# Two attention decode blocks, last heads of an output projection: loaded in long rows, laid out, and summed in four column groups

## The chip, the core and the metric

One core of a Trainium2 chip runs the whole kernel. The metric is device time in microseconds (us), the median of several runs; a profile of one execution stands beside it. Engines are named as in the profile: PE (matmul; PEld its weight loads), DVE (vector), ACT (scalar), POOL and SP (it issues most DMAs here).

## What is computed

Two independent blocks, A and B, of single-token attention with caches, of 32 heads, 8192 cached positions and 128 dimensions each; the outputs stand side by side (1 x 1 x 1024):

```python
q = (x @ wq).reshape(1, 1, 32, 128).transpose(0, 2, 1, 3)
scores = jnp.einsum("bhqd,bhkd->bhqk", q, k_cache) * 128 ** -0.5
p = softmax(scores, axis=-1)
o = jnp.einsum("bhqk,bhkd->bhqd", p, v_cache)
y = o.transpose(0, 2, 1, 3).reshape(1, 1, 32 * 128) @ wo        # wo: 4096 x 512
# out = concatenate([y of A, y of B], axis=-1)
```

All inputs are bf16. Each of the four caches has 67 MB, each `wq` and `wo` 4.2 MB.

## The kernel before, in words

The engines' programs are written out by hand, one stream an engine, with semaphores between them. Four heads form a group; 16 groups (8 of A, 8 of B) go through a loop on PE, DVE and ACT each. One group has 8.4 MB of K and 8.4 MB of V. K has two slots in `kn`, V one in `vn`; SP issues the loads in order, each behind the semaphore that frees its slot. In a round DVE multiplies K by q in place (L279), PE adds over the dimensions with matmuls on an identity (L430), DVE reduces to scores (L307) and their maximum, ACT takes the exponential (L379), PE multiplies by V (L483), DVE adds up the four parts of PE's result (L284, L287), PE sums over the partitions (`total_of_group`, L436), and DVE divides (`outs`, L296).

`wo` of A and of B go into the K slot that is free at the end. The loads are issued by SP behind the last V load: A in one piece, B in six, `WOB` (L89). A piece with `rows` true is read as `(p j) n -> p (j n)`: partition p gets `j` whole rows of `wo` in one run, so that with j = 4 it is 4 KB. In this form the rows of one head lie on 128/j partitions, so the heads' outputs have to be laid out accordingly: `spread` (L328, DVE) multiplies them with a mask into `zb`, PE multiplies by a selection `jsel` (L449, `mid`), and `lay` (L336, DVE) copies the result into `o2`. That is done for all heads but the last four, ahead of the last V group. The last four heads of B, 28 to 31, come as three loads in plain rows of 1 KB (2, 1 and 1 heads), and their outputs go straight from the division into `o2` (L347).

Heads of A and heads 0 to 15 of B are multiplied with `wo` by `partial` (L443): 512 columns at a time, head h into column group h mod 4 of `yps[0]` (partitions 0, 32, 64, 96), two rows (A, B) each. ACT copies that to `yc` (L382, semaphore c_ya). Then PE adds the four groups with a selection matrix `sel16`, for A and B at once, into two column groups of `yps[1]` of 256 columns (L496), and adds heads 16 to 31 of B there, two matmuls a head (L505). The last of them raises c_y. DVE copies one half to `out_sb` (L349, c_yd) and ACT the other (L384, c_ya); SP waits for both and stores 2 KB (L232). `turn_over` (L461) are five matmuls without use of their results, between the two parts.

Of the kernel before, what the change touches and what calls it, by code (L numbers as in the profile page):

```python
# [8 lines left out]
BF16 = mybir.dt.bfloat16  # L9
F32 = mybir.dt.float32  # L10

P = 128
# [33 lines left out]
def bass_concat_heads__mha_block_cached__gqa_block_cached__decode_kernel(  # L46
# [41 lines left out]

    WOB = [(0, 16, True), (16, 8, True), (24, 4, True), (28, 2, False), (30, 1, False), (31, 1, False)]  # L89
    RG = [32, 16, 8, 4]  # L90
    NH = NOUT // 2

    with ExitStack() as st:
# [3 lines left out]
        def sb(name, shape, dt):  # L97
            return ec(nc.sbuf_tensor(name, shape, dt))
# [56 lines left out]

        c_pool, c_sel, c_mul, c_sr, c_g, c_gm, c_self, c_st, c_o, c_rl, c_yd = (
            sem(n) for n in ("c_pool", "c_sel", "c_mul", "c_sr", "c_g", "c_gm", "c_self", "c_st", "c_o", "c_rl", "c_yd"))

# [28 lines left out]
        def _(e):  # L187
# [20 lines left out]
            def load_wob(g):  # L208
                h0, n, rows = WOB[g]
                src = wos[1][h0 * Dh:(h0 + n) * Dh, :]  # L210
                dst = kn[:, WO + h0 * NOUT:WO + (h0 + n) * NOUT]
                if rows:
                    src = src.rearrange("(p j) n -> p (j n)", p=P)
                elif n > 1:
                    src = src.rearrange("(j p) n -> p j n", p=P)
                    dst = dst.rearrange("p (j n) -> p j n", j=n)
                e.dma_start(dst, src).then_inc(s_wob[g], 16)

# [13 lines left out]
            e.dma_start(out[0].rearrange("o (a n) -> (o a) n", a=NA), out_sb[:]).then_inc(s_out, 16)  # L232
            e.wait_ge(s_out, 16)
# [9 lines left out]
        def _(e):  # L243
            with once(e):
# [48 lines left out]
                def outs(dst):  # L293
                    w_self()
                    w_ex()
                    e.tensor_tensor(dst, mtp[:, EX:EX + G], rinv[:], ALU.mult).then_inc(c_o, 1)  # L296
# [22 lines left out]

                todo = [(0, 0, H)] + [(1, h0, n) for h0, n, rows in WOB if rows]  # L320
                e.wait_ge(c_o, N)
# [19 lines left out]
                spread(1)  # L341
                for i in range(len(todo)):
                    lay(i)
                    if i + 2 < len(todo):
# [4 lines left out]
                e.tensor_copy(out_sb[:, 0:NH], yps[1][0:NA, 0:NH]).then_inc(c_yd, 1)  # L349


        @block.scalar
        def _(e):
            load_wq(e, 1)
            with once(e):
# [26 lines left out]
                e.copy(yc, yps[0][:]).then_inc(c_ya, 1)  # L382
                e.wait_ge(c_y, 2)
                e.copy(out_sb[:, NH:NOUT], yps[1][HP:HP + NA, 0:NH]).then_inc(c_ya, 1)  # L384


        @block.tensor
        def _(e):
            with once(e):
# [48 lines left out]
                def wo_rows(h):  # L438
                    return kn[:, h * NOUT:(h + 1) * NOUT]

                def partial(h):
                    k = h % G * HP
                    return e.matmul(yps[0][k:k + NA, :], o2[:, h, :], wo_rows(h), start=False, stop=False,  # L443
                                    skip_group_check=True)

                def mid():
                    for i, (a, h0, n) in enumerate([(0, 0, H)] + [(1, h0, n) for h0, n, rows in WOB if rows]):
                        e.wait_ge(c_rl, (1, 2, 4, 6)[i])
                        e.matmul(lay_ps[i][:, 0:n], zb[:, i % 2, :], jsel[n][:], start=True,  # L449
                                 stop=True).then_inc(c_rm, 1)  # L450
# [43 lines left out]
                e.wait_ge(c_ya, 1)  # L494
                for b in range(2):
                    e.matmul(yps[1][b * HP:b * HP + NA, 0:NH], sel16[:, 0, 0:NA],  # L496
                             yc[:, b * NH:(b + 1) * NH], start=True, stop=False, skip_group_check=True)
                for g in range(1, len(WOB)):
                    h0, n, rows = WOB[g]
                    e.wait_ge(s_wob[g], 16)  # L500
                    for h in range(h0, h0 + n):
                        for b in range(2):
                            if h == H - G - 1 and b:
                                e.wait_ge(c_o, N + 1)
                            m = e.matmul(yps[1][b * HP:b * HP + NA, 0:NH], o2[:, H + h, :],  # L505
                                         wo_rows(H + h)[:, b * NH:(b + 1) * NH], start=False,
                                         stop=(h == H - 1), skip_group_check=True)
                m.then_inc(c_y, 1)

# [27 lines left out]
```

## Time and profile before

| | |
|---|---|
| time, median of 3 runs | 665.04 us (664.96 to 666.86) |
| span of the profiled execution, first to last instruction | 663.5 us |
| median over that span | 1.5 us |
| mean granted PE clock in the span | 0.792 |
| DMA read | 285.2 MB, 430 GB/s over the span |
| PE, DVE, ACT busy | 58%, 55%, 12% |

The profiled execution's own time is its span of 663.5 us; what lies around it is not in the profile, and the runs' median is 1.5 us above it. Busy shares are over the whole span. A row of the timeline gives start, length, engine, line, operation, output and input, count, and in brackets the idle time ahead and what ended it; matmul ends are modelled, and consecutive matmuls overlap. Rows of the windows give the stretch, the busy time and count of each engine, the granted PE clock, the DMA engines' share and GB/s. Lines are those of the kernel before.

### The profile page before, as it was taken

Reading aid. Unit: us, or ns where it says so; the run is one execution under the profiler, and the core shown is the slowest. Engines: PE = TensorE matmul, PEld = TensorE weight load, DVE = VectorE, ACT = ScalarE, POOL = GpSimd, SP = SyncE. Lnnn points to the kernel's source line nnn. Section 1 sums busy time; section 2 is a strip of 40 time slices with the busy share of each in tenths; the row PEclk is TensorE's granted clock in tenths of the full one; section 3 lists DMA queues with packets and bytes.
Section 4 is the critical chain, followed back from the end, with each engine's and each line's share of the span. In section 5 each row is a group of like instructions: output and inputs, shape, how many; then the busy total and the mean of one; then the engine's idle time right before and its main releaser. Section 6 shows DMA issues by size and latency. Waiting matters only on the chain.

```text
span 663.5 us, 7942 instructions
## 1 busy us (share of the span) xinstructions
PE 385.8 (58%) x2402; PEld 191.8 (29%) x2402; DVE 362.5 (55%) x249; ACT 76.6 (12%) x212; POOL 2.3 (0%) x12
## 2 busy tenths in 40 slices
PE   0455685854819185481918548191854819185488
PEld 0122232423315042330404233140423314032233
DVE  1009494848292754829274482927548292744821
ACT  0370202020010202001020200102020010202002
POOL 1000000000000000000000000000000000000000
PEclk9995988786959678695967869596786959678697
DMA  9999998999999999999999999999999999999997
GB/s 379 443 442 442 442 442 379 442 442 442 442 442 442 391 431 442 442 442 442 442 399 423 442 442 442 442 442 411 411 442 442 442 442 442 415 407 442 440 444 317
DMA packets 6041, 285.23 MB, mean 430 GB/s; under 512 B 660, under 2 KB 1176, under 8 KB 1304
## 3 DMA queue, kind: packets, MB, share of 16 engines
q1 hardware_dynamic: 5896, 281.03, 98.0%
q10 hardware_dynamic: 144, 4.19, 1.5%
q14 instruction: 1, 0.01, 0.0%
HBM read 285.21 MB, written 0.00 MB: 430 GB/s over the span
## 4 chain that ended last, share of the span: by engine, by line
DMA 72%; PE 22%; DVE 2%; issue 2%; ACT 1%; ACTq 0%; DVEq 0%; SPq 0%
DMA vn<-in_B_v_cache_dram 34%; DMA vn<-in_A_v_cache_dram 34%; PE acc L483 14%; PE rps L430 5%; DMA xrow<-in_B_x_dram 3%; PE yps L413 2%; DVE kn L279 1%; ACT qmem L368 1%; PE yps L443 1%; ACT pt L379 0%; PE yps L505 0%; DVE s_sb L307 0%; PE rps L461 0%; PE misc L478 0%; PE rps L424 0%
## 5 line engine op out<-in xcount | busy, mean ns | idle before, releaser
L279 DVE TENSOR_TENSOR kn<-kn,qmem 128x16384 bf16<-128x16384 bf16 x32 | 276.7, 8688 | 55.2 <-ACT qmem L368 43.0
L430 PE MATMUL rps<-kn,ident 128*128 x1024 | 236.8, 383 | 0.4
L483 PE MATMUL acc<-vn,pt 128*32 128x512 bf16 x1024 | 92.3, 531 | 145.7 <-DMA vn<-in_B_v_cache_dram 75.3
L307 DVE TENSOR_REDUCE s_sb<-rps 128x64 f32<-128x512 f32 x64 | 44.1, 691 | 165.1 <-PE rps L430 165.1
L430 PEld LDWEIGHTS rps<-kn,ident 128*128 128x128 bf16 x1024 | 96.4, 98 | 111.0 <-issue 22.6
L483 PEld LDWEIGHTS acc<-vn,pt 128*32 128x32 bf16 x1024 | 60.3, 127 | 171.1 <-issue 155.9
L374 ACT ACTIVATE negb<-bmp 128x4 f32<-128x4 f32 x16 | 2.8, 173 | 539.7 <-PE bmp L472 539.7
L379 ACT ACTIVATE pt<-s_sb,negb 32x256 bf16<-32x256 f32 x64 | 54.9, 858 | 4.3 <-ACT negb L374 2.9
L478 PE MATMUL misc<-rsum,ones_f 128*128 128x4 f32 x32 | 9.4, 365 | 56.4 <-ACT pt L379 56.4
L284 DVE TENSOR_SCALAR om<-acc,msk 128x128 f32<-128x128 f32 x16 | 5.6, 350 | 42.8 <-PE acc L483 42.8
L478 PEld LDWEIGHTS misc<-rsum,ones_f 128*128 128x128 f32 x32 | 8.0, 312 | 58.6 <-ACT pt L379 57.8
L413 PE MATMUL yps<-vn,xT 128*128 x64 | 17.3, 419 | 6.2 <-ACT qmem L368 4.2
L287 DVE SCALAR_TENSOR_TENSOR om<-acc,msk,om 128x128 f32<-128x128 f32 x48 | 16.8, 351 | 5.9
L470 PE MATMUL mtp<-ident_f,m 128*1 128x128 f32 x32 | 6.1, 270 | 22.6 <-DVE m L312 22.6
L424 PE MATMUL rps<-ones_bf,zrow 1*128 1x1 bf16 x64 | 11.0, 171 | 13.4 <-DVE kn L279 10.8
L424 PEld LDWEIGHTS rps<-ones_bf,zrow 1*128 1x128 bf16 x64 | 5.8, 91 | 40.6 <-issue 40.6
L368 ACT CAST qmem<-yps 32x128 f32 x64 | 16.4, 256 | 7.0 <-PE yps L413 6.3
L379 ACT ACTIVATION_READ_ACCUMULATOR pt<-s_sb,negb 32x1 f32 x64 | 15.9, 249 | 0.0
L399 PE MATMUL misc<-ident,xrow 2*128 2x2 bf16 x4 | 0.3, 166 | 22.8 <-DMA xrow<-in_B_x_dram 22.8
L413 PEld LDWEIGHTS yps<-vn,xT 128*128 x64 | 6.6, 103 | 16.5 <-issue 13.7
L472 PE MATMUL bmp<-gm,ones_f 1*128 1x4 f32 x32 | 6.1, 258 | 7.3 <-DVE gm L314 7.3
L470 PEld LDWEIGHTS mtp<-ident_f,m 128*1 128x1 f32 x32 | 1.4, 80 | 30.5 <-DVE m L312 30.5
(58 smaller groups left out, 57.0 us busy)
## 6 DMA issues: line engine op xcount, KB each, us to landing
vn<-in_B_wq_dram ACTq DMA_DIRECT2D x1, 4096.0 KB, 21.9
vn<-in_A_wq_dram SPq DMA_DIRECT2D x1, 4096.0 KB, 21.7
kn<-in_A_wo_dram SPq DMA_DIRECT2D x1, 4096.0 KB, 27.4
kn<-in_B_wo_dram SPq DMA_DIRECT2D x1, 2048.0 KB, 27.7
kn<-in_B_wo_dram SPq DMA_DIRECT2D x1, 1024.0 KB, 29.7
kn<-in_B_wo_dram SPq DMA_DIRECT2D x1, 512.0 KB, 30.5
kn<-in_B_wo_dram SPq DMA_DIRECT2D x1, 256.0 KB, 30.8
kn<-in_B_wo_dram SPq DMA_DIRECT2D x2, 128.0 KB, 30.6
```

The source lines that it names most:

```text
L279: e.tensor_tensor(k, k, qflat[:, bass.ds(q, Dh)].unsqueeze(1).broadcast_to([P, HM, Dh]), ALU.mult).then_inc(c_mul, 2)
L287: e.scalar_tensor_tensor(om[t % 2][:], acc[:, t * Dh:(t + 1) * Dh], msk[:, t:t + 1], om[(t + 1) % 2][:], ALU.mult, ALU.add).then_inc(*((c_ ...
L307: e.tensor_reduce(s_sb[:, h * HT:(h + 1) * HT], rps[:, h % 2, :].rearrange("p (t d) -> p t d", d=DW), AX.X, ALU.add).then_inc(c_sr, 1)
L368: i = e.copy(qflat[p, bass.ds(r * (2 * Dh) + j * Dh, Dh)], yps[j][p, h * Dh:(h + 1) * Dh])
L379: e.activation(pt[p, 0:T, h], s_sb[p, :], AF.Exp, bias=negb[p, h:h + 1], scale=scale, accum_out=rsum[p, h:h + 1]).then_inc(c_p, 4)
L413: i = e.matmul(yps[j][:], xT[:, bass.ds(x0 + c, 1)].broadcast_to([P, P]), vn[:, bass.ds(w0 + (c * H * Dh + j * G * Dh), G * Dh)], start=(c ...
L424: e.matmul(rps[:, tile, 0:1], zrow[:], ones_bf[0:1, 0:1], start=True, stop=False, skip_group_check=True)
L430: m = e.matmul(ro, ident[:], src, start=False, stop=False, skip_group_check=True)
L443: return e.matmul(yps[0][k:k + NA, :], o2[:, h, :], wo_rows(h), start=False, stop=False, skip_group_check=True)
L470: e.matmul(mtp[0:1, 0:P], m1[:], ident_f[:], start=True, stop=True).then_inc(c_gx, 1)
L478: e.matmul(misc[:, 0:G], ones_f[:], rsum[:], start=True, stop=True)
L483: m = e.matmul(acc[k:k + HP, :], ptf[:, g * W * G:g * W * G + HP], vn[:, g * W * Dh:(g + 1) * W * Dh], start=(g < G), stop=(g >= NG - G))
```

## The change

- The last four heads of `wo` of B are one load of 4 KB rows. Their outputs are laid out like the others: division into `oD`, `spread`, matmul into `bmp`, `lay`.
- Heads 16 to 31 of B are multiplied in four column groups of 128 columns, one row (B) each, in place of two groups of 256 columns with two rows.
- The four column groups of the first part are added for A and B apart (`total`): B into `yps[1]` ahead of heads 16 to 23, A into the second bank of `rps` ahead of the last four heads.
- ACT copies both results, A first, from four partitions (0, 32, 64, 96; the copy covers 97) with 128 columns each; DVE copies none, and c_yd is gone. The store takes four partitions with two runs of 128 each.

```diff
-    WOB = [(0, 16, True), (16, 8, True), (24, 4, True), (28, 2, False), (30, 1, False), (31, 1, False)]
+    WOB = [(0, 16), (16, 8), (24, 4), (28, 4)]
-    NH = NOUT // 2
+    NQ = NOUT // 4
-        out_sb = sb("out_sb", [NA, NOUT], BF16)
+        out_sb = sb("out_sb", [P, NA * NQ], BF16)
-        lay_ps = [misc, yps[1], acc, mtp]
+        lay_ps = [misc, yps[1], acc, mtp, bmp]
# SP
-            e.wait_ge(c_yd, 1)
-            e.wait_ge(c_ya, 2)
-            e.dma_start(out[0].rearrange("o (a n) -> (o a) n", a=NA), out_sb[:]).then_inc(s_out, 16)
+            e.wait_ge(c_ya, 3)
+            e.dma_start(out[0].rearrange("o (a b n) -> b (o a) n", a=NA, b=G),
+                        out_sb[0:P:HP, :].rearrange("b (a n) -> b a n", a=NA)).then_inc(s_out, 16)
# DVE
                 part()
-                outs(o2[:, NA * H - G:NA * H, NA - 1])
-                e.wait_ge(c_y, 2)
-                e.tensor_copy(out_sb[:, 0:NH], yps[1][0:NA, 0:NH]).then_inc(c_yd, 1)
+                outs(oD[:, N * G:N * G + G])
+                e.wait_ge(c_o, N + 1)
+                spread(last)
+                lay(last)
# ACT
-                e.wait_ge(c_y, 2)
-                e.copy(out_sb[:, NH:NOUT], yps[1][HP:HP + NA, 0:NH]).then_inc(c_ya, 1)
+                for a, t in enumerate((rps[:, 1, :], yps[1][:])):
+                    e.wait_ge(c_y, 2 + a)
+                    e.copy(out_sb[0:P - HP + 1, a * NQ:(a + 1) * NQ], t[0:P - HP + 1, 0:NQ]).then_inc(c_ya, 1)
# PE
+                def layout(i):
+                    n = ns[i]
+                    e.wait_ge(c_rl, (1, 2, 4, 6, 9)[i])
+                    e.matmul(lay_ps[i][:, 0:n], zb[:, i % 2, :], jsel[n][:], start=True,
+                             stop=True).then_inc(c_rm, 1)
...
-                for b in range(2):
-                    e.matmul(yps[1][b * HP:b * HP + NA, 0:NH], sel16[:, 0, 0:NA],
-                             yc[:, b * NH:(b + 1) * NH], start=True, stop=False, skip_group_check=True)
+                def total(a, t):
+                    for b in range(G):
+                        m = e.matmul(t[b * HP:b * HP + 1, 0:NQ], sel16[:, 0, a:a + 1],
+                                     yc[:, b * NQ:(b + 1) * NQ], start=True, stop=(a == 0),
+                                     skip_group_check=True)
+                    return m
...
+                def piece(g):
+                    h0, n = WOB[g]
                     e.wait_ge(s_wob[g], 16)
                     for h in range(h0, h0 + n):
-                        for b in range(2):
-                            if h == H - G - 1 and b:
-                                e.wait_ge(c_o, N + 1)
-                            m = e.matmul(yps[1][b * HP:b * HP + NA, 0:NH], o2[:, H + h, :],
-                                         wo_rows(H + h)[:, b * NH:(b + 1) * NH], start=False,
+                        for b in range(G):
+                            m = e.matmul(yps[1][b * HP:b * HP + 1, 0:NQ], o2[:, H + h, 1:2],
+                                         wo_rows(H + h)[:, b * NQ:(b + 1) * NQ], start=False,
                                          stop=(h == H - 1), skip_group_check=True)
-                m.then_inc(c_y, 1)
+                    return m
+
+                total(1, yps[1])
+                piece(1)
+                layout(len(ns) - 1)
+                piece(2)
+                total(0, rps[:, 1, :]).then_inc(c_y, 1)
+                e.wait_ge(c_rl, 10)
+                piece(3).then_inc(c_y, 1)
```

The end of PE's program, from the sum over the column groups on (`sel` is `sel16`, `qmem` holds `yc`, `o` is `o2`; s_wob0 to s_wob5 are the landings of the pieces of `wo` of B; in brackets what an instruction waits for). Before:

```order
L496 MATMUL yps<-qmem,sel 2x256
L505 MATMUL yps<-kn,o 2x256 [waits s_wob1]
L505 MATMUL yps<-kn,o 2x256 x15
L505 MATMUL yps<-kn,o 2x256 [waits s_wob2]
L505 MATMUL yps<-kn,o 2x256 x6
L505 MATMUL yps<-kn,o 2x256 [waits c_o]
L505 MATMUL yps<-kn,o 2x256 [waits s_wob3]
L505 MATMUL yps<-kn,o 2x256 x3
L505 MATMUL yps<-kn,o 2x256 [waits s_wob4]
L505 MATMUL yps<-kn,o 2x256
L505 MATMUL yps<-kn,o 2x256 [waits s_wob5]
L505 MATMUL yps<-kn,o 2x256
```

And now, with lines of the changed kernel:

```order
L502 MATMUL yps<-qmem,sel 1x128 [waits c_ya]
L502 MATMUL yps<-qmem,sel 1x128 x3
L512 MATMUL yps<-kn,o 1x128 [waits s_wob1]
L512 MATMUL yps<-kn,o 1x128 x31
L449 MATMUL bmp<-jsel,zb 128x4 [waits c_rl]
L512 MATMUL yps<-kn,o 1x128 [waits s_wob2]
L512 MATMUL yps<-kn,o 1x128 x15
L502 MATMUL rps<-qmem,sel 1x128 x4
L512 MATMUL yps<-kn,o 1x128 [waits s_wob3,c_rl]
L512 MATMUL yps<-kn,o 1x128 x15
```

Heads 16 to 31 take 64 matmuls where they took 32, a layout stands ahead of heads 24 to 27, the sum for A stands ahead of the last four heads, and one landing (s_wob3) stands where there were three.

The end of DVE's program, from the reciprocal of the last group on (`oD` holds the divided outputs, `zb` the spread ones, c_y is PE's last result). Before:

```order
L287 SCALAR_TENSOR_TENSOR om<-acc,msk,om 128x128
L291 RECIPROCAL rinv<-misc 128x4 [waits c_o]
L296 TENSOR_TENSOR o<-mtp,rinv 128x4 [waits c_ex,c_self]
L349 CAST out_sb<-yps 2x256 [waits c_y]
L244 REGISTER_ALU
```

And now:

```order
L286 RECIPROCAL rinv<-misc 128x4 [waits c_o]
L291 TENSOR_TENSOR oD<-mtp,rinv 128x4 [waits c_ex,c_self]
L324 TENSOR_TENSOR zb<-oD,mask 128x128 [waits c_rm,c_o]
L332 CAST o<-bmp 128x4 [waits c_rm]
L239 REGISTER_ALU
```

The copy of the result is gone from DVE's end, and a multiply and a small copy for the last four heads stand there.

More of the change, by code (lines that the diff above doesn't have):

```diff
@@ L154, in bass_concat_heads__mha_block_cached__gqa_block_cached__decode_kernel @@
         s_k = [sem("s_k%d" % i) for i in range(2)]
-        c_pool, c_sel, c_mul, c_sr, c_g, c_gm, c_self, c_st, c_o, c_rl, c_yd = (
-            sem(n) for n in ("c_pool", "c_sel", "c_mul", "c_sr", "c_g", "c_gm", "c_self", "c_st", "c_o", "c_rl", "c_yd"))
+        c_pool, c_sel, c_mul, c_sr, c_g, c_gm, c_self, c_st, c_o, c_rl = (
+            sem(n) for n in ("c_pool", "c_sel", "c_mul", "c_sr", "c_g", "c_gm", "c_self", "c_st", "c_o", "c_rl"))
         c_qa, c_nb, c_p, c_ya = (sem(n) for n in ("c_qa", "c_nb", "c_p", "c_ya"))
@@ L208, in load_wob @@
             def load_wob(g):
[L209 to L217, printed above, removed]
+                h0, n = WOB[g]
+                e.dma_start(kn[:, WO + h0 * NOUT:WO + (h0 + n) * NOUT],
+                            wos[1][h0 * Dh:(h0 + n) * Dh, :].rearrange("(p j) n -> p (j n)", p=P)
+                            ).then_inc(s_wob[g], 16)
             load_k(0)
@@ L317, in _ @@
                         outs(oD[:, bass.ds(r * G, G)])
-                todo = [(0, 0, H)] + [(1, h0, n) for h0, n, rows in WOB if rows]
+                todo = [(0, 0, H)] + [(1, h0, n) for h0, n in WOB]
+                last = len(todo) - 1
                 e.wait_ge(c_o, N)
@@ L341, in _ @@
                 spread(1)
-                for i in range(len(todo)):
+                for i in range(last):
                     lay(i)
-                    if i + 2 < len(todo):
+                    if i + 2 < last:
                         spread(i + 2)
                 part()
-                outs(o2[:, NA * H - G:NA * H, NA - 1])
-                e.wait_ge(c_y, 2)
-                e.tensor_copy(out_sb[:, 0:NH], yps[1][0:NA, 0:NH]).then_inc(c_yd, 1)
+                outs(oD[:, N * G:N * G + G])
+                e.wait_ge(c_o, N + 1)
+                spread(last)
+                lay(last)
         @block.scalar
@@ L444, in partial @@
                                     skip_group_check=True)
+                ns = [H] + [n for h0, n in WOB]
+                def layout(i):
[3 more added lines that the diff above has]
+                             stop=True).then_inc(c_rm, 1)
                 def mid():
[L447 to L450, printed above, removed]
+                    for i in range(len(ns) - 1):
+                        layout(i)
                     e.matmul(yps[0][:], zrow[:], ones_bf[0:1, 0:1].broadcast_to([1, 512]), start=True,
```

3 lines of the change are left out of this document (1 added, 2 removed).

## The prediction

> **What bounds the kernel now.** I read the page's first parts, then the chain of work that ended last, then the timeline of the last microseconds.
>
> ```profile
> span 663.5 us, 7942 instructions
> PE 385.8 (58%) x2402; PEld 191.8 (29%) x2402; DVE 362.5 (55%) x249; ACT 76.6 (12%) x212; POOL 2.3 (0%) x12
> DMA  9999998999999999999999999999999999999997
> DMA 72%; PE 22%; DVE 2%; issue 2%; ACT 1%; ACTq 0%; DVEq 0%; SPq 0%
> q14 instruction: 1, 0.01, 0.0%
> ```
>
> The DMA engines are full in every slice but the last, and 72% of the chain is DMA: the caches stream in at the pace of the memory, and nothing that the change touches lies in that stream. All of it lies behind the last cache block. So I price only the tail, from the chain in order of time and the timeline (start, length, engine, line; in brackets the idle time before and who ended it).
>
> ```profile
> 652.58 4.28 PE acc L483 x46
> 656.87 0.86 PE yps L443 x11
> 657.73 1.19 PE rps L461 x5
> ```
> ```profile
> 656.70 1.03 PE L443 MATMUL yps<-kn,o 128*2 128x512 bf16 x16
> ...
> 658.76 0.38 PE L436 MATMUL mtp<-selh,om 128*128 128x4 f32 x2
> ...
> 659.08 0.60 PE L496 MATMUL yps<-qmem,sel 128*2 128x256 f32 x4
> 659.25 0.16 DVE L296 TENSOR_TENSOR o<-mtp,rinv 128x4 bf16<-128x4 f32 x1 [0.46 <-PE mtp L436]
> 659.29 1.40 PEld L505 LDWEIGHTS yps<-kn,o 128*2 128x2 bf16 x24
> 659.51 2.37 PE L505 MATMUL yps<-kn,o 128*2 128x256 bf16 x32
> 660.94 0.09 PEld L505 LDWEIGHTS yps<-kn,o 128*2 128x2 bf16 x4 [0.25 <-DMA kn<-in_B_wo_dram]
> 661.31 0.08 PEld L505 LDWEIGHTS yps<-kn,o 128*2 128x2 bf16 x2 [0.28 <-DMA kn<-in_B_wo_dram]
> 661.60 0.08 PEld L505 LDWEIGHTS yps<-kn,o 128*2 128x2 bf16 x2 [0.21 <-DMA kn<-in_B_wo_dram]
> 661.92 0.36 ACT L384 CAST out_sb<-yps 2x256 bf16<-2x256 f32 x1 [3.55 <-PE yps L505]
> 661.92 0.41 DVE L349 CAST out_sb<-yps 2x256 bf16<-2x256 f32 x1 [2.50 <-PE yps L505]
> 662.37 0.27 SPq L232 DMA_DIRECT2D out_dram<-out_sb  x1
> ```
>
> The chain calls the end PE work without a gap from 652.58 on. The timeline tells more: the reader is to see three short waits for `wo` of B, before heads 28 and 29, before 30 and before 31 (660.94, 661.31, 661.60), 0.7 us together. The last one decides: 0.32 us later (661.92) the copies begin, the longer ends at 662.33, the store is issued at 662.37 and the span ends at 663.5. The whole stretch that can change is 659.1 to 663.5, 4.4 us. The sum is made against this execution: span 663.5; the runs' median, 665.04, lies 1.5 us above it, and I carry differences of the span over to it.
>
> **Part 1, the last four heads in one load of 4 KB rows.** Three loads in 1 KB rows become one. The rate in stretches of 8 KB rows, 4 KB rows and 1 KB rows, in that order (the last number is GB/s):
>
> ```profile
> 655.90:658.00 2.10, 2.10 (x38) 0.81 (x31) 0.82 (x3) 0.21 (x1) 0.00 (x0) 1.00 1.01 421
> 658.40:659.30 0.90, 0.90 (x9) 0.42 (x8) 0.44 (x3) 0.00 (x0) 0.00 (x0) 1.00 1.02 411
> 659.65:660.65 1.00, 1.00 (x24) 0.84 (x20) 0.00 (x0) 0.00 (x0) 0.00 (x0) 1.00 1.11 363
> ```
>
> The last 524 KB take 524/363 = 1.44 us as 1 KB rows and 524/411 = 1.28 us as 4 KB rows: the last byte is 0.16 us earlier, so PE is released at 661.45 in place of 661.60. Bounds: no gain if the end is set by a fixed completion time, 0.2 us at most. I take -0.15. SP issues two loads fewer; it had issued all of them 30 us before they were needed, so that counts nothing.
>
> What is lost is that work could begin on parts. Before, 2 matmuls stood behind the last landing; now 16 do (4 heads by 4 column groups). For their pace I have two rows. In L443, also four column groups, the last of 16 matmuls ends 0.38 us after its start, so three steps of four matmuls with 512 columns take 1.03 - 0.38 = 0.65 us, 0.217 a step; at 128 columns that is 0.054 a head. From above, the shortest matmuls of the trace:
>
> ```profile
> 22.76 0.21 PEld L399 LDWEIGHTS misc<-ident,xrow 2*128 2x128 bf16 x4 [22.76 <-issue]
> 22.79 0.26 PE L399 MATMUL misc<-ident,xrow 2*128 2x2 bf16 x4 [22.79 <-DMA xrow<-in_B_x_dram]
> L399 PE MATMUL misc<-ident,xrow 2*128 2x2 bf16 x4 | 0.3, 166 | 22.8 <-DMA xrow<-in_B_x_dram 22.8
> ```
>
> Four of 2 columns take 0.26 us, the last 0.17 of it: 0.03 a matmul with its weights, 0.12 to 0.13 a head of four. Before, 24 weight loads, 12 heads, take 1.40 us, 0.12 a head. I take 0.06, near L443, which has the same column groups. Three heads then stand between release and the last one: +0.18 (0.16 to 0.39). The last matmul itself is shorter: 512 columns are recorded at 379 ns and 256 at 272, so 128 are about 218, -0.05.
>
> ```profile
> L443 PE MATMUL yps<-kn,o x48: 379/631/634, 648.5 to 657.4; 128*2 128x512 bf16 x48
> L505 PE MATMUL yps<-kn,o x32: 270/272/273, 659.5 to 661.6; 128*2 128x256 bf16 x32
> ```
>
> **Part 2, laying these heads out.** DVE now runs one more multiply and one more copy and PE a matmul between them. The same steps of the earlier groups:
>
> ```profile
> 646.28 0.16 DVE L296 TENSOR_TENSOR oD<-mtp,rinv 128x4 f32 x1 [0.91 <-PE mtp L436]
> 646.52 0.49 DVE L328 TENSOR_TENSOR zb<-oD,mask 128x128 bf16<-128x128 bf16 x2
> 646.88 0.19 PE L449 MATMUL misc<-jsel,zb 128*128 128x32 bf16 x1 [0.75 <-DVE zb L328]
> 647.10 0.20 DVE L336 CAST o<-misc 128x32 bf16<-128x32 f32 x1
> ```
>
> From the head division to the spread heads is 646.28 to 647.30, 1.02 us. From 659.25 this ends at 660.27 if PE is free at once. On PE it stands behind the total for B and heads 16 to 23. The total: L496's four passes hold PE from 659.08 to 659.51; half the columns in four groups take about half, to 659.30. Eight heads at 0.06 end at 659.78, at 0.13 at 660.34. The new wait of PE (for DVE's multiply, ready at 659.25 + 0.60 = 659.85) holds up heads 24 to 27 and the total for A behind it, by 0.1 us; the layout matmul costs 0.2. Heads 24 to 27 then run from about 660.2, when their 4 KB rows have come, to 660.5 (slow pace 661.2), the total for A to 660.7 (661.5). All that has the wait for the last rows, 661.45, as its cover: 0.7 us to spare at the pace I take, none at the slow one. Where the cover is gone (slow pace, and 0.2 us at each of three changes between kinds of matmul, most of the 0.32 from L436's start to L496's, in which L436 has two passes of 4 columns), the last piece starts near 661.9, ends at 662.6, and the span is 0.5 longer. I count 0 and keep 0.5.
>
> **Part 3, one copy and the store.** DVE's copy of 0.41 us and ACT's of 0.36 become two of ACT, of which one runs while PE waits. The other has 128 columns:
>
> ```profile
> L368 ACT CAST qmem<-yps x64: 254/256/258, 27.0 to 47.7; 32x128 f32 x64
> ```
>
> 0.25 for 0.41: -0.16. ACT's first copy (0.25) ends by 661.0; at the slow pace by 661.8, still before 661.9. The store moves 2 KB as eight rows of 256 B from four partitions in place of two of 1 KB. No row shows a store like it. What is there is 0.27 us of issue and a final wait:
>
> ```profile
> SPq L233 <- DMA out_dram<-out_sb: 0.9, 1, 0.9
> ```
>
> Bounds: -0.05 (shorter rows over more engines) to one issue more, +0.27; I take +0.05, near the row, as the bytes are the same. [...]
>
> **Sum.** -0.15 + 0.18 - 0.05 + 0 - 0.16 + 0.05 = -0.13 us: span 663.4, time 664.9. The bounds of these terms, with the PE case, are -0.3 to +0.8: 664.7 to 665.8. The runs of before themselves reach from 664.96 to 666.86; with that I set the lower end at 664.4.
>
> **Rivals.**
> *Slower: PE's program outgrows what it keeps at hand.* Counted over the order (loops once, a matmul with its weight load as two, an fp32 one as four) PE has 443 instructions before and 534 after; the 91 are all at the end: 8 fp32 and 64 bf16 matmuls, a layout and a wait for 2 and 32 of before (32 + 128 + 2 + 1 - 8 - 64). The row of q14 speaks against: one instruction packet in the whole span, while PE's loop ran 16 times; all 443 stayed at hand. It says nothing of 534. It decides if the room lies between 443 and 534: then the last piece waits for a fetch. Its price from rows: 1.2 us (662.37 to 663.5, the round trip of a small transfer) to 2.7 (that, behind the 1.5 us of `wo` that are still under way). 666.1 to 667.6; more if it also empties the loop's own start, for which no row has a price. [...]
> [...]
> *The change doesn't do what it says:* the last rows land no earlier, since a completion time and not the rows sets 661.60. Then the term of -0.15 goes: 665.05. Against it: the waits of 660.94, 661.31 and 661.60 come 0.3 to 0.4 apart, and 131 KB at 363 GB/s take 0.36, so the rate sets them.
> Faster by 2 us would need the chain from 661.45 to 663.5 to vanish; no term reaches it.
>
> **How the numbers follow.** Forecast, 664.9 within its bounds: 0.58. Landing no earlier: 0.07. The store's second trip: 0.07. Room for the program: 0.26, of which 0.14 for one fetch (666.1 to 667.6) and 0.12 for more. Faster by chance of the 660 us ahead of the tail: 0.02. The range 664.3 to 667.4 leaves out the 0.12, the 0.02 and some 0.05 at its two ends; the forecast alone would have 664.4 to 665.8. A difference within 0.3%, 2.0 us, is about what a measurement of this kernel can tell from no change. Over 667.04 lie the 0.12 and about 0.05 of the single fetch: slower 0.17. Faster 0.02, same 0.81.
>
> **What would show it.** Right: one wait for `wo` of B before the last 16 matmuls, ending near 661.4; those 16 within 0.25 us; a last ACT copy of 0.25; the store issued near 662.2; q14 still at one packet. Wrong: 16 matmuls over 0.4 us apart (pace); PE busy without a wait for DMA before the last piece (cover gone); a final wait on the store over 1.5 us (second trip); instruction packets inside the span with PE idle behind no semaphore (room).

## The result: 2.5 us slower, by a late DMA engine and a store that took twice as long

The changed kernel takes 667.50 us (median of 5 runs, 667.19 to 669.55), the kernel before in the same session 665.04 us (5 runs, 664.96 to 666.86): a ratio of 1.0039, 95% interval 1.0028 to 1.0049. That is outside the forecast range of 664.3 to 667.4 by 0.1 us, and on the side (slower) to which the prediction gave 0.17. The profiled execution of the changed kernel took 667.38 us, with a span of 666.1 against 663.5.

The page of the changed kernel: the span, the DMA engines in 40 slices, the rows of the instruction queues (packets, MB, share) and the chain.

```profile
span 666.1 us, 8028 instructions
...
DMA  9999998999999999999999999999999999999996
...
q8 instruction: 1, 0.02, 0.0%
q14 instruction: 1, 0.01, 0.0%
...
DMA 77%; PE 16%; issue 3%; ACT 1%; DVE 1%; SPq 0%; ACTq 0%; DVEq 0%
```

The DMA engines are still full up to the last slice. One row is new: an instruction packet of queue q8. Where it is, and what follows the next load, is in the trace's DMA view for 86 to 89 us and for 99.9 to 101.0 us:

```profile
q1 hardware_dynamic: 16, 1.05, 81.8%
q8 instruction: 1, 0.02, 2.0%
```
```profile
DMA packets 2, 0.07 MB, mean 60 GB/s; under 512 B 1, under 2 KB 1, under 8 KB 1
```

The packet of q8 has 16,384 B, starts at 87.39 us and lasts 0.95 us. Of the 16 data packets of 65,536 B that end at 87.29 to 87.59 us, 15 are followed by the next one by 87.58; one has no successor before 88.32, when the instruction packet is nearly over (88.34). The traces do not name the 16 DMA engines; I read this as one of them being held. In the next load, 15 landing marks come by 99.82 us; one data packet and its mark are still to come, at 100.90. From there on one landing in 16 comes 0.95 to 1.08 us behind the other 15 in every cache load up to 632 us; one of the last big loads ends at 623.33 us (15 of its marks by 622.28). Before, all 16 came within 0.5 us, and that load ended at 621.93: 1.40 earlier. At the end of the program the windows show it plainly; the last two numbers are the DMA engines' share and GB/s. The changed kernel first, then the kernel before:

```profile
661.40:662.30 0.90, 0.61 (x24) 0.32 (x24) 0.00 (x0) 0.00 (x0) 0.00 (x0) 1.00 0.07 27
```
```profile
661.40:662.30 0.90, 0.46 (x4) 0.08 (x2) 0.38 (x1) 0.36 (x1) 0.00 (x0) 1.00 0.00 0
```

A share of 0.07 is one engine of 16: it alone is still loading, while before there was nothing left to load. The timeline of the changed kernel's end:

```profile
657.89 0.53 PEld L441 LDWEIGHTS yps<-kn,o 128*2 128x2 bf16 x16 [0.36 <-DMA kn<-in_B_wo_dram]
...
660.24 0.40 PE L502 MATMUL yps<-qmem,sel 128*1 128x128 f32 x8
...
660.41 0.16 DVE L291 TENSOR_TENSOR oD<-mtp,rinv 128x4 bf16<-128x4 f32 x1 [0.46 <-PE mtp L434]
660.45 0.63 PE L512 MATMUL yps<-kn,o 128*1 128x128 bf16 x32
660.61 0.29 DVE L324 TENSOR_TENSOR zb<-oD,mask 128x128 bf16<-128x128 bf16 x1
661.01 0.10 PEld L449 LDWEIGHTS bmp<-jsel,zb 128*128 128x128 bf16 x1
661.01 0.18 PE L449 MATMUL bmp<-jsel,zb 128*128 128x4 bf16 x1
661.23 0.17 DVE L332 CAST o<-bmp 128x4 bf16<-128x4 f32 x1 [0.33 <-PE bmp L449]
...
661.66 0.40 PE L512 MATMUL yps<-kn,o 128*1 128x128 bf16 x16 [0.47 <-DMA kn<-in_B_wo_dram]
...
662.95 0.39 PE L512 MATMUL yps<-kn,o 128*1 128x128 bf16 x16 [0.67 <-DMA kn<-in_B_wo_dram]
663.39 0.27 ACT L382 CAST out_sb<-yps 97x128 bf16<-97x128 f32 x1 [0.78 <-PE yps L512]
663.68 0.65 SPq L226 DMA_DIRECT2D out_dram<-out_sb  x1
```

The reader is to see two things. PE now waits for `wo` of B before heads 0 to 15 already (657.89), and again before heads 24 to 27 and 28 to 31: nothing of PE's own is in the way, only the late engine. And the store's issue takes 0.65 us, not 0.27. SP's final wait on the store, from the view of waits, is 1.7 us where it was 0.9:

```profile
SPq L228 <- DMA out_dram<-out_sb: 1.7, 1, 1.7
```

The two profiled executions against each other, in us (the landing is the last 4-byte mark of the last load, the first matmul counts from its weight load, the copy's start is that of the last ACT copy, and the end is the start of SP's last wait instruction, 0.02 us before the span ends):

| | before | after | difference |
|---|---|---|---|
| last landing | 661.09 | 662.31 | +1.22 |
| to the first matmul behind it | 0.51 | 0.61 | +0.10 |
| to the last copy's start | 0.32 | 0.47 | +0.15 |
| to the store's issue (the copy) | 0.45 | 0.29 | -0.16 |
| from the issue to the end | 1.16 | 2.41 | +1.25 |
| span | 663.55 | 666.11 | +2.56 |

So two numbers are to be explained: 1.2 us at the landing (the 1.40 of the stream, less 0.18 for the faster last rows) and 1.25 us at the store. The rest, on which most of the prediction's working went, comes to +0.09. Single traces of one kernel differ in the last landing, but the two kinds do not overlap: in the eight traces of this document with a q8 packet near 87 us it comes at 662.31 to 663.32, in the nine without one at 661.04 to 661.88.

### The profile page after: what moved, and what is told of

Same layout as the page of the kernel before. It is cut to its first block, busy times and chain, and to the rows that moved or that the text cites. A ratio compares the mean times of both kernels' runs of the same rounds, so it can differ in the third digit from the quotient of the medians.

```text
span 666.1 us, 8028 instructions
## 1 busy us (share of the span) xinstructions
PE 380.8 (57%) x2442; PEld 190.9 (29%) x2447; DVE 362.6 (54%) x250; ACT 76.8 (12%) x213; POOL 2.3 (0%) x12
## 4 chain that ended last, share of the span: by engine, by line
DMA 77%; PE 16%; issue 3%; ACT 1%; DVE 1%; SPq 0%; ACTq 0%; DVEq 0%
DMA vn<-in_A_v_cache_dram 35%; DMA vn<-in_B_v_cache_dram 35%; PE acc L487 13%; DMA kn<-in_B_wo_dram 5%; DMA xrow<-in_B_x_dram 3%; PE yps L411 2%; PE rps L428 1%; ACT qmem L365 1%; DVE kn L274 1%; ACT pt L376 0%; DVE s_sb L302 0%; SPq L210 0%; ACTq L365 0%; ACTq L43 0%; PE misc L482 0%
## 5 line engine op out<-in xcount | busy, mean ns | idle before, releaser
L487 PE MATMUL acc<-vn,pt 128*32 128x512 bf16 x1024 | 88.4, 514 | 148.8 <-DMA vn<-in_B_v_cache_dram 76.8
L291 DVE TENSOR_TENSOR oD<-mtp,rinv 128x4 f32 (+1 forms) x16 | 2.6, 162 | 14.1 <-PE mtp L434 14.1
```

The source lines that it names most:

```text
L487: m = e.matmul(acc[k:k + HP, :], ptf[:, g * W * G:g * W * G + HP], vn[:, g * W * Dh:(g + 1) * W * Dh], start=(g < G), stop=(g >= NG - G))
```

## The experiments on the late DMA engine

My theory: PE's longer program is fetched in part, and the fetch costs no stall of PE but the place of one DMA engine in the stream. The rival: the changed loads or the new matmuls at the end make the lag. Instructions are counted as in the prediction, 443 before and 534 after; times are medians, with the difference to the kernel before in the same session.

**Code that never runs, at the end of PE's program before.**

```diff
                 m.then_inc(c_y, 1)
+                with e.If(e.snap(by_round) == 1):
+                    for i in range(46):
+                        e.matmul(rps[:, 0, 0:1], ident[:], kn[:, 0:1], start=True, stop=True)
```

With 46 such matmuls (538 instructions):

> The kernel before, with 46 matmuls at the end of PE's program in a branch that is never taken: PE's program grows by 95 instructions to 538 and does nothing more. Theory (the program's length costs a fetch inside the span, whose 16 KB packet sets one of the 16 DMA engines back for good): one instruction packet of 16 KB in the span, one landing of each load about 1.3 us after the other 15, time 666.3 us (+1.3). Rival (the lag of the changed kernel comes from its loads or its timing): no such packet, 665.0.

Measured: 666.21 us (665.98 to 667.65), +1.03, ratio 1.0017 (1.0008 to 1.0026); the packet is there, at 87.17 us, and one landing in 16 is late as in the changed kernel:

```profile
q8 instruction: 1, 0.02, 0.0%
```

So length alone does it, without one instruction more being executed but the branch. With 20 matmuls (486 instructions):

> The same branch with 20 matmuls: 486 instructions, between before (443) and the change (534). [...] If any code added at the end costs a fetch, or the branch itself costs time: 666.3.

Measured: 666.18 us (665.96 to 666.91), +1.00, ratio 1.0017 (1.0008 to 1.0026), with the same packet at 87.26 us. So the limit, if the length sets it, lies below 486.

**The changed kernel without heads 16 to 23 of B** (470 instructions):

```diff
                 total(1, yps[1])
-                piece(1)
                 layout(len(ns) - 1)
```

> The changed kernel without the products of heads 16 to 23 of B (they are left out of the sum): 470 instructions on PE. These matmuls stand in the cover of a landing, so that leaving them out saves nothing by itself. Theory: no packet in the span, the last landing 1.3 us earlier, 666.2 us (667.5 before this edit). Rival (lag from the one long load or from chance): 667.5.

Measured: 667.52 us (667.29 to 668.24), +2.34; the packet is at 87.22. That is the time which the rival foretold. It does not bring the rival back, since the padded kernels have the lag without any change of loads; with the length as the cause, the limit lies below 470. With 4 matmuls of padding, 454:

> The kernel before with 4 matmuls behind a condition that is never true at the end of PE's program: 454 instructions by my count. The packet comes between 443 (none) and 470 (there). If the limit lies near 448: a 16 KB instruction packet near 87 us and one landing of 16 about 1.3 us behind, time about 666.2. If it lies at 460 or more: none, 665.2.

Measured, in one execution: no packet near 87 us and all 16 landings together, span 664.2. But the time was 668.8, 4.6 us more than the span, and a 16 KB packet of q8 stands at 666.17, 2.0 us behind the span's end. So, if the count alone decides, the limit for the fetch inside the stream lies between 454 and 470. The packet behind the end is taken up below.

**The changed kernel without heads 16 to 27 of B** (438 instructions, fewer than before):

```diff
                 total(1, yps[1])
-                piece(1)
                 layout(len(ns) - 1)
-                piece(2)
                 total(0, rps[:, 1, :]).then_inc(c_y, 1)
```

> The changed kernel without the products of heads 16 to 27 of B (left out of the sum): 438 instructions on PE, five fewer than before. All loads, the layout, the last four heads, the copies and the store stay. Theory (the fetch comes with any program longer than that of before): no packet of 16 KB in the span, no landing behind the others, 667.5 - 1.2 = 666.3 us; the store still takes 2.4 us. Rival (the fetch belongs to the changed program's form): packet and 667.5.

Measured: 666.93 us (666.31 to 667.78), +1.86, ratio 1.0027 (1.0017 to 1.0037). In the profiled execution the packet of q8 is gone from the stream, all 16 landings come together again (the last at 661.09 us, as in the kernel before), and the span is 665.1, 1.0 less than after. The median is 0.6 above the expected 666.3, which only the four shortest runs show (666.31 to 666.44): in the others up to 2.35 us lie around the span, where the runs of the kernel before in that session had 1.2 to 1.5. In the trace a q8 packet stands at 666.48, behind the span.

Such a packet behind PE's last branch stands in five traces: with 4 matmuls of padding, without heads 16 to 27 (here, and in the run below with the store of zeros), and in two forms of the changed kernel below, the one that stores zeros and the one in which DVE makes the last copy. Where it lies behind the span (the first, this one and the changed kernel that stores zeros), 4.6, 2.0 and 2.0 us lie around the span; in the other 13 profiled executions whose time is known beside their span, 1.2 to 1.4. That the late packet lengthens the end fits these, but no run tests it; and what makes it come is open: of the kernels with 534 instructions two have it and two do not.

**The loop's hint left out** (the kernel before, 442 instructions; each engine's whole program stands in a loop of one round that was marked as jumping back):

```diff
-            return nc.Fori(0, e.snap(one), engines=[e.engine], hint_back_edge=True)
+            return nc.Fori(0, e.snap(one), engines=[e.engine])
```

> The kernel before with its loop's hint on the back edge left out on all engines (442 instructions on PE by my count). Theory A, the fetch is a matter of the program's length alone: no packet near 87 us, 665.1 +- 0.4. Theory B, the hint is what keeps the loop's code at hand at 443 instructions: packets of instructions inside the span, 666 or more.

Measured: 666.16 us (665.98 to 667.47), +1.00, ratio 1.0015 (1.0006 to 1.0025). Both queues now fetch inside the stream, q14 at 82.53 and q8 at 87.25 us, two of the 16 landings are late (by 0.8 and 1.3 us), and no packet follows at the end. So length is not all: at nearly the same length the hint decides too.

## The experiments on the store

**The changed kernel with a store of two runs of 1 KB,** from a tile of zeros, the result's copies unchanged:

```diff
+            e.memset(out_2k[:], 0.0).then_inc(c_pool, 1)
...
-            e.dma_start(out[0].rearrange("o (a b n) -> b (o a) n", a=NA, b=G),
-                        out_sb[0:P:HP, :].rearrange("b (a n) -> b a n", a=NA)).then_inc(s_out, 16)
+            e.dma_start(out[0].rearrange("o (a n) -> (o a) n", a=NA), out_2k[:]).then_inc(s_out, 16)
```

> The changed kernel with the store of before: two rows of 1 KB, from a tile of zeros, so that the result itself is not stored. All waits stay. Theory (short rows and their number make the store 1.25 us longer, 2.41 from issue to the end for 1.16): 667.5 - 1.25 = 666.25 us. Rival (the store was late for SP's own instruction packet, which stood ahead of it): 667.4.

Measured: 666.13 us (665.93 to 667.64), +0.95, ratio 1.0017 (1.0008 to 1.0026); the store takes 1.17 us again, and the late engine remains (last landing at 663.04). With the store alone changed, 1.4 to 1.5 us are gone.

**Both costs taken away** (without heads 16 to 27, and the store of zeros):

> The same, with the store of before (two rows of 1 KB from a tile of zeros; the result itself is not stored). Theory: both costs gone, and what is left is the change as forecast: 665.0 us within 0.3, last landing 0.15 earlier than before. Rival (a third cost, in the tail's work): 665.8 or more.

Measured: 665.45 us (664.84 to 665.89), +0.38, ratio 1.0004 (0.9995 to 1.0013). Within what a measurement can tell, that is the kernel before: the two costs are nearly the whole loss. In its trace the last landing is not 0.15 earlier, as I had expected, but 0.79 later than in the kernel before (661.88); all 16 came together, and the load that ended at 621.93 there ends at 622.43 here, so most of this lag was there before the tail began.

**What in the store?** First I held the short runs responsible. In the kernel before, with `out_sb` padded so that the two partitions give eight runs of 256 B:

```diff
-            e.dma_start(out[0].rearrange("o (a n) -> (o a) n", a=NA), out_sb[:]).then_inc(s_out, 16)
+            e.dma_start(out[0].rearrange("o (a b n) -> (o a) b n", a=NA, b=G), out_sb[:, :, 0:P]).then_inc(s_out, 16)
```

> The kernel before, with its two result rows padded in the on-chip tile, so that the same two partitions are stored as eight runs of 256 B. [...] Rival (four partitions, not short rows, cost it): 665.2.

Measured: 666.45 us (666.02 to 667.98), +1.38; store 2.30 us. And with four runs of 512 B (`b=2`, halves of 256 columns):

> The same with a pad after 256 columns: four runs of 512 B. [...] Rival (each run costs, whatever its length): about a third of the way, 665.6.

Measured: 666.35 us (666.11 to 667.29), +1.28; store 2.41 us. Runs of 512 B cost as much as runs of 256 B, so I took the length not to be it. What the length alone costs these two stores do not tell, since both met the fetch that is found further down; a store of 256 B runs that did not meet it is shown there (1.73 us, 0.02 us a run). Then the form, three dimensions in place of two? The changed kernel with one run of 512 B from each of the four partitions (in two dimensions, the columns landing in another order):

```diff
-            e.dma_start(out[0].rearrange("o (a b n) -> b (o a) n", a=NA, b=G),
-                        out_sb[0:P:HP, :].rearrange("b (a n) -> b a n", a=NA)).then_inc(s_out, 16)
+            e.dma_start(out[0].rearrange("o (b n) -> (o b) n", b=G), out_sb[0:P:HP, :]).then_inc(s_out, 16)
```

> The changed kernel, but its 2 KB leave as four runs of 512 B, one from each of the four partitions (a plain form of two dimensions), in place of eight runs of 256 B in three dimensions; they land in another order. The instruction packet at 87 us remains. Theory 1, the form of the transfer costs the 1.2 us (its issue, 0.65 to 0.78 us): issue 0.27, store 1.2 us, time 666.2 +- 0.3 (as with two runs of 1 KB, 666.13). Theory 2, the number of runs or partitions costs it: store 2.3 to 2.5 us, time 667.4 +- 0.3.

Measured: 667.90 us (667.50 to 668.25), +2.74; issue 0.60, store 2.49 us. Not the dimensions either.

**The variant that should have had no loss** kept the last four heads in 4 KB rows and in four column groups, but with two result rows a group, heads 16 to 27 multiplied like heads 0 to 15 (512 columns at a time), without the five matmuls of `turn_over`, with four copies (two of DVE, two of ACT) and the old store of two runs of 1 KB. Of its edit:

```diff
-            e.wait_ge(c_ya, 3)
-            e.dma_start(out[0].rearrange("o (a b n) -> b (o a) n", a=NA, b=G),
-                        out_sb[0:P:HP, :].rearrange("b (a n) -> b a n", a=NA)).then_inc(s_out, 16)
+            e.wait_ge(c_yd, 1)
+            e.wait_ge(c_ya, 2)
+            e.dma_start(out[0].rearrange("o (a n) -> (o a) n", a=NA), out_sb[:]).then_inc(s_out, 16)
...
-                        for b in range(G):
-                            m = e.matmul(yps[1][b * HP:b * HP + 1, 0:NQ], o2[:, H + h, 1:2],
...
+                    for b in range(G):
+                        m = e.matmul(yps[1][b * HP:b * HP + NA, 0:NQ], o2[:, H + h, :],
...
```

> What the change brought, without its two costs: the last four heads of wo of B in one load of 4 KB rows, laid out, in four column groups of 128, but with two rows a group; heads 16 to 27 as the first 16 (512 columns); four copies into two partitions, store of two runs of 1 KB. PE has 440 instructions by my count (before 443). Theory (fetch and store are the whole loss): no instruction packet near 87 us, all 16 landings of a load together, store 1.2 us, 665.0 +- 0.4: no gain over before beyond what a measurement tells. Rival (the tail itself is slower): 665.8 or more.

Measured: 666.80 us (666.12 to 667.20), +1.64, ratio 1.0023 (1.0014 to 1.0032). No fetch of PE, all landings together, and yet the loss remains. Two rows of its timeline and one of its waits tell why:

```profile
661.38 0.60 PE L511 MATMUL yps<-qmem,sel 128*2 128x128 f32 x8 [0.69 <-ACT qmem L383]
...
663.07 0.27 SPq L227 DMA_DIRECT2D out_dram<-out_sb  x1
```
```profile
SPq L228 <- DMA out_dram<-out_sb: 2.0, 1, 2.0
```

PE waits for ACT's copy of the column sums, which now comes behind heads 24 to 27 (the store is issued 0.7 us later than before). But above all, the very store that took 1.16 us before, with its issue of 0.27, takes 2.31 us here. With this the theory of the store's form falls as the whole cause.

**A new theory.** I laid the packets of these stores beside each other, in us from the store's issue (data: start of the first and the last data packet; zeros: the changed kernel that stores zeros; four copies: the variant just shown):

```
                     issue  q14's packet     first data  last data  end
before               0.27   +1.16 to +1.66   +0.74       +0.77      +1.16
zeros, 2 x 1 KB      0.27   +1.19 to +1.64   +0.74       +0.78      +1.17
after, 8 x 256 B     0.65   +1.25 to +1.60   +1.28       +1.61      +2.41
without heads 16-27  0.65   +1.54 to +1.85   +1.28       +1.86      +2.70
before, 8 x 256 B    0.78   +1.14 to +1.62   +1.42       +1.66      +2.30
before, 4 x 512 B    0.78   +1.15 to +1.63   +1.41       +1.65      +2.41
after, 4 x 512 B     0.60   +1.26 to +1.77   +1.23       +1.77      +2.49
four copies          0.27   +0.94 to +1.49   +0.74       +1.49      +2.31
```

In each store of over 2 us the last data goes out within 0.04 us of the end of q14's packet of 8 KB, as if it had waited for it. In the two stores of 1.2 us the data is through before. And q14's packet comes 1.41 to 1.48 us after the end of ACT's branch out of its loop (1.70 in one case), whatever PE, DVE and SP do. So my theory: q14 is ACT's instruction queue, its packet is a fetch of ACT once out of its loop, and the store loses a place to that fetch. ACT leaves when its last copy has started (in the changed kernel the copy starts at 663.39 us and the branch ends at 663.53), so the fetch, at 664.94, falls where the store goes out (first data at 664.96). Three runs test it against the form of the store.

**The changed kernel with DVE making the last copy,** store unchanged:

```diff
+                e.wait_ge(c_y, 3)
+                e.tensor_copy(out_sb[0:P - HP + 1, NQ:2 * NQ], yps[1][0:P - HP + 1, 0:NQ]).then_inc(c_yd, 1)
...
-                for a, t in enumerate((rps[:, 1, :], yps[1][:])):
-                    e.wait_ge(c_y, 2 + a)
-                    e.copy(out_sb[0:P - HP + 1, a * NQ:(a + 1) * NQ], t[0:P - HP + 1, 0:NQ]).then_inc(c_ya, 1)
+                e.wait_ge(c_y, 2)
+                e.copy(out_sb[0:P - HP + 1, 0:NQ], rps[0:P - HP + 1, 1, 0:NQ]).then_inc(c_ya, 1)
```

> The changed kernel, its store of eight runs of 256 B and PE's fetch at 87 us as they are; only the last copy (128 columns) is DVE's in place of ACT's, so that ACT leaves its loop about 1.0 us earlier. Theory 1, ACT's fetch at its loop's end stands in the store's way: the packet of q14 comes near 663.9, a microsecond before the store's packets; store 1.7 us from issue to end (first packet 1.28, the rest 0.1, then 0.34 to SP) in place of 2.41; time 666.8 +- 0.3. Theory 2, the form of the store alone: store 2.4 us, time 667.5 +- 0.3.

Measured: 666.93 us (666.57 to 669.48), +1.68, ratio 1.0036 (1.0021 to 1.0050); span 665.7. q14 starts at 664.11 us, 1.45 after the end of ACT's branch, and is over at 664.52; the data goes out from 665.23 to 665.32, and the store takes 1.73 us, as the new theory has it.

```profile
663.57 0.29 DVE L349 CAST out_sb<-yps 97x128 bf16<-97x128 f32 x1 [1.93 <-PE yps L514]
663.95 0.65 SPq L227 DMA_DIRECT2D out_dram<-out_sb  x1
```
```profile
SPq L229 <- DMA out_dram<-out_sb: 1.1, 1, 1.1
```

The issue is still 0.65, the wait behind it 1.1 in place of 1.7. That splits the 1.25 us: 0.57 (1.73 against 1.16) belong to the store's own form, with a first packet at +1.28 in place of +0.74; 0.68 (2.41 against 1.73) to meeting the fetch. The split rests on one trace of each. Each of the eight runs of 256 B takes 0.02 us here, and SP's wait ends 0.36 us after the last mark, 0.34 in the kernel before: of the second trip to which the prediction gave 0.07 there is no sign.

The DMA view of this kernel from 662 to 667 us also has a packet of PE's queue:

```profile
q8 instruction: 1, 0.02, 1.3%
```

It lasts from 664.69 to 665.76 us, over the whole time of the store's data, and holds none of it (nor does one at 663.64 to 664.57 us in the kernel with both costs taken away). So a fetch at the same moment is not enough. That both must fall on the same DMA engine is my guess; the traces do not name the engines.

**The variant with four copies, all of them on DVE:**

> The variant with four copies and a store of two runs of 1 KB (666.8, store 2.31), with all four copies on DVE: 0.57 us more of copying on the path, and ACT leaves its loop after the copy of the column sums, near 660.8. Theory 1 (ACT's fetch): q14 near 662.2, the store takes 1.16 us again, time 666.8 + 0.57 - 1.15 = 666.2 +- 0.3. Theory 2 (something else in this variant's store): 2.3 us, 667.4 +- 0.3.

Measured: 666.73 us (665.83 to 668.22), +1.48, ratio 1.0023 (1.0014 to 1.0031). q14 goes to 662.54 us and the store takes 1.17 us.

```profile
662.64 1.18 DVE L348 CAST out_sb<-yps 2x128 bf16<-2x128 f32 x4 [2.67 <-PE yps L512]
663.85 0.27 SPq L226 DMA_DIRECT2D out_dram<-out_sb  x1
```
```profile
SPq L227 <- DMA out_dram<-out_sb: 0.9, 1, 0.9
```

The store is as foretold, the time is not: 0.2 above the expected range. The copies ended 0.8 us later (0.6 for the copies, 0.2 for PE's result) and the store 1.1 shorter; the span's median over the runs fell only from 665.4 to 665.0, and the median time hardly.

**The kernel before, its store a little later:** DVE's copy of 256 columns in four of 64.

```diff
-                e.tensor_copy(out_sb[:, 0:NH], yps[1][0:NA, 0:NH]).then_inc(c_yd, 1)
+                for b in range(4):
+                    i = e.tensor_copy(out_sb[:, b * NH // 4:(b + 1) * NH // 4],
+                                      yps[1][0:NA, b * NH // 4:(b + 1) * NH // 4])
+                i.then_inc(c_yd, 1)
```

> The kernel before with DVE's last copy of 256 columns cut into four of 64, so that the same store of two runs of 1 KB is issued 0.4 to 0.5 us later and ACT's fetch stays where it is (about 1.45 us after ACT's branch). Theory 1 (ACT's fetch): the store's packets meet the fetch, the store takes 2.2 to 2.4 us in place of 1.16, time 665.1 + 0.45 + 1.1 = 666.7 +- 0.4. Theory 2 (the form of the store alone): 1.16 us, time 665.6 +- 0.3.

Measured: 666.36 us (665.14 to 667.63), +1.11, ratio 1.0017 (1.0008 to 1.0026).

```profile
662.03 0.60 DVE L350 CAST out_sb<-yps 2x64 bf16<-2x64 f32 x4 [2.52 <-PE yps L508]
662.67 0.27 SPq L232 DMA_DIRECT2D out_dram<-out_sb  x1
```
```profile
SPq L233 <- DMA out_dram<-out_sb: 2.1, 1, 2.1
```

The copies take 0.2 us longer, less than I had put in, and the same store of two runs of 1 KB takes 2.36 us: first data at +0.75, q14's packet from +1.20 to +1.51 (this time 1.70 us after ACT's branch), last data at +1.51. Nothing about the store has changed but its moment. The meeting alone costs 1.2 us here, more than the delay that brings it about.

One thing does not fit a plain queue behind the packet. The second data packet was due at +0.77, as before, and q14's packet begins 0.43 us later: the data is held ahead of the packet's own record. Counted from the end of ACT's branch, second packets of such a store that went out up to 1.10 us behind it were free (six traces), and those due at 1.26 and 1.27 us (the variant with four copies, and this kernel) were held. The kernel before, at 1.09, escapes by less than 0.2 us. What holds the engine in that time is not in the trace.

## Why the prediction was wrong, point by point

- **Landing of the last rows, -0.15.** The rate was right: the marks of one engine for the last 524 KB lie 1.25 to 1.27 us apart, about 1.45 before, -0.18. The step that failed is the premise under this term, that nothing the change touches lies in the stream of the caches. The change made PE's program longer, and an instruction packet came into that stream at 87.39 us: from there on one landing of 16 was 0.95 to 1.08 us behind, and the last landing came 1.22 later. In the padded kernels that packet is worth about 1.0 us of time. (The row of slices that I read as full up to the last also has one 8; nothing hangs on that.)
- **The rival on PE's program.** It had the right condition, a limit between 443 and 534 (454 to 470, if the count alone decides), and 0.26. Its price was wrong: a stall of PE before the last piece, 1.2 to 2.7 us. The runs show no such stall, but the lag of one engine. That its span of times, 666.1 to 667.6, takes in the measured 667.50 is luck: half of the loss came from the store.
- **The row of q14.** I read it as PE's own record, which showed that all 443 instructions stayed at hand. It was ACT's: it moves with ACT's branch (the copies on DVE) and not with PE's, and it stands at 663.54, in the last 0.02 us of the span. PE's queue is q8: code on PE alone, never run, made it appear. The row spoke neither for nor against.
- **The size of that room.** That PE keeps a certain number of instructions at hand was my own picture; the runs show only when a packet comes, not what PE holds. The packet has 16,384 B, and the limit for it in the stream lies between 454 and 470 by my count, if the count alone decides. The changed kernel has one packet in 16 rounds, at 87.39 us, and none when PE leaves its loop for the code behind it. Whether that packet brings code for the first time or again is not in the traces, so that they give no size of a room.
- **Pace, +0.18 and -0.05.** 16 matmuls take 0.39 us, one 0.22: 0.17 for the steps, 0.13 for three heads (forecast 0.18). Right, a little generous.
- **Layout, 0.** From the division at 660.41 to the laid-out heads at 661.40 is 0.99 us (forecast 1.02), and behind it PE waited 0.47 and 0.67 us for DMA. The cover held. The late engine does not explain that: it held up PE's start into this stretch (657.89, before 656.70) by as much as the last landing. The whole kernel without the lag was not tried.
- **Copy, -0.16.** 0.265 us in place of 0.41. Right.
- **Store, +0.05.** This term failed as well. "The bytes are the same" was the reason, and the bounds ended at one issue more, +0.27. It was +1.25: 0.57 for a longer issue and a later first packet, 0.68 for meeting ACT's fetch. A second trip, which has 0.07 among the chances, is shown by no run: without the fetch each run of 256 B took 0.02 us, and SP's wait ended 0.36 us after the last mark (0.34 in the kernel before). Its sign, a final wait on the store over 1.5 us, came (1.7) and meant something else. Nor does any run show shorter rows going over more engines, the reason given for the lower bound of -0.05.
- **The range.** It reached to 667.4 by way of a single fetch, so that it missed by only 0.1 us is no merit of the sum. That lag and a slow store would both come was not among the cases; each was priced as if the other did not exist.

## What to carry to other kernels

In a kernel whose DMA engines are full, ask of every longer program whether it brings an instruction packet into the stream: here it came with 534 instructions on PE by my count (not with 443), stalled no engine (PE's next matmuls ran from 87.53 us, while the packet lasted to 88.34), but left one landing of 16 behind by 0.95 to 1.08 us in every cache load up to 632 us, and the last landing came 1.22 us later than before. At the end of a program look at what else is on the DMA engines just then: here the instruction packet of q14 came 1.41 to 1.48 us (1.70 in two cases) behind ACT's branch out of its loop (with the loop's hint), and a store that met it paid 0.7 to 1.2 us, so let that engine be done early, or the store be out first. The small transfer of this kernel was priced by its moment and its issue, not by its bytes.

No version here beats the kernel before in time. What the change wins in the tail itself, 0.18 for the rows and 0.16 for the copy, less 0.25 between landing and copy, is about 0.1 us, which no measurement of this kernel would show.

## What the runs showed of the hardware

- Fetches of PE are one packet of 16 KB (0.93 to 1.08 us long), those of ACT one of 8 KB (0.31 to 0.55 us). In the eight kernels with PE's in the stream it comes once, at 87.07 to 87.41 us, 0.55 to 1.41 us after the end of the branch that closes the first round of PE's loop; why there, and in none of the 15 rounds behind it, stays open.
- In this full stream the late landing of the 16 did not catch up: 1.08 us behind the last of the other 15 at 100.90 us, 1.05 at 623.33.
- An issue of a store cost SP 0.27 us for two runs of 1 KB, 0.60 for four partitions with 512 B each, 0.65 for four with two of 256 B, 0.78 for two partitions with two or four runs; the first packet follows 0.47 to 0.64 us after that issue's end.
- In the stores that met the fetch SP's last wait ends 0.63 to 0.83 us after the last mark, in those of 1.2 us 0.34. That this, too, comes from the fetch is shown, in one trace, by the store that no longer met it (0.36, with its issue still 0.65); by what mechanism is open.
